# Output copies moved ahead of normalization and decoding in an attention pass, and its small transfers moved from GpSimd's queue to SyncE's

## The chip, the cores and the metric

One core of a Trainium2 chip runs the whole kernel. The metric is device time in microseconds, the median of the runs. TensorE is called PE here, VectorE DVE, ScalarE ACT, GpSimd POOL and SyncE SP, as in the profile.

## The reference

Attention with capped scores over 2 batches, 12 heads, 448 positions and 64 columns a head, and then two feed-forward stages on the 896 by 768 result:

```python
scores = cap * np.tanh(scale * np.matmul(q, k.transpose(0, 1, 3, 2)) / cap)
attn = np.exp(scores - np.max(scores, axis=-1, keepdims=True))
attn = attn / (np.sum(attn, axis=-1, keepdims=True) + 1e-09)
x = heads_side_by_side(np.matmul(attn, v))        # 896 x 768
h = x @ w_in                                      # 768 -> 2048
x = (h * (1.0 / (1.0 + np.exp(-1.702 * h)))) @ w_out
xn = x / np.sqrt(np.mean(x * x, axis=-1, keepdims=True) + 1e-06) * rms_g
g = xn @ w_gate                                   # 768 -> 1536
return (g * (1.0 / (1.0 + np.exp(-g))) * (xn @ w_val)) @ w_out2
```

## The kernel before

The order of the instructions on every engine is the order of the program text, so each engine works through its own list, and one instruction that waits holds up all that stand behind it on that engine.

**Attention.** Two heads make a pair; there are 12 pairs (`NPR`), and the loop over `p` runs 13 times (passes 0 to 12). Pass `p` holds work of several pairs. On PE, in this order: the last 64 rows of the scores of pair p (`scores_last`, L305), the transposes of q and k of pair p+1 (`turn`, L263), most of the product of weights and values of pair p-1 (`pv_main`, L332), the third block of scores of pair p and the first of pair p+1 (`scores`, L295), the end of the product of pair p-1 (`pv_last`, L342), and the second block of scores of pair p+1. ACT takes tanh and exp of each block (`exps`, L317 and L318; `tt` are the large blocks, `tl` the last one). PSUM banks rotate: the tiles `v` of `scores_last` and of the two heads of `pv_main` share two banks, three tiles to a pass. So `scores_last` of a pass waits for the output copy of head 0 of the pass before (`z`, L350, on DVE), and the second head of `pv_main` waits until ACT has taken the tanh of `tl` out of the bank that `scores_last` of the same pass filled.

**Normalization.** The values carry a column of ones, so each output `z` holds the sums of its softmax. `sums` spreads those sums over partitions into `rs` by a DMA; `recips` inverts them on DVE (L364) and, for pairs 0 to 8, writes them to DRAM (`recs`, L367); `spread` reads them back to all partitions of a tile `r` (L382), 224 KB written from 3.5 KB. These three transfers are on POOL's queue for pairs 0 to 8. For pairs 9 to 11 the spreading is a product with `blk` on PE (L386). `normal` (L393, L399, L405) multiplies and splits the result in a high and a low part on DVE. In pass p it is the turn of `recips` and `spread` of pair p-3 and, right behind them, of `normal` of pair p-4, ahead of the output copies of pair p-1 on DVE's list. The spreadings of pairs 9 and 10 share one PSUM tile (`spare`).

**Decoding.** Weights of the feed-forward stages come as raw words (`raw`), and each unit of six blocks is decoded by `square`, `sign`, `mask` on ACT, `mid`, `top`, `low` on DVE, `high_part` on ACT (L158) and `low_part` on DVE (L163). Operations of units 0 to 3 are spread over passes 3 to 12 in the order of the list `early`, two in the middle of a pass and one at its end. `low` of a unit also issues the load of the unit three further on, on SP's queue.

**SP's queue** carries the loads of q, k, v and raw weights.

**Feed-forward stages.** They begin with the columns of batch 0 (L558 to L560) right behind the last product of attention, the spreading of pair 10.

Of the kernel before, what the change touches and what calls it, by code (L numbers as in the profile page):

```python
# [9 lines left out]
F32 = mybir.dt.float32  # L10
F32R = mybir.dt.float32r
# [7 lines left out]
def attn_moe_kernel(  # L19
# [14 lines left out]
    nc = tc.nc  # L34
    B, H, S, D = q.shape
# [8 lines left out]
    NPR = B * NP  # L44
# [120 lines left out]
    def run(op, w):  # L165
        if w < len(units) and (op, w) not in done:
            done.add((op, w))
            op(w)
# [8 lines left out]
    def attention():  # L177
        with ExitStack() as actx:
# [89 lines left out]
            def split_kq(p):  # L268
                t, ts = turned.pop(p)
                if p:  # L270
                    x = ap_.tile([128, 2, 2, S], F32R, tag="x", name="x")
                    xs[p] = [[x[:, a, j] for j in range(2)] for a in range(2)]
                    nc.vector.tensor_copy(x[:, 0], t[:, :, 0:S])  # L273
                    nc.vector.tensor_tensor(out=x[:, 1], in0=t[:, :, 0:S], in1=f(x[:, 0]), op=ALU.subtract)
                    for e in range(2):
                        nc.gpsimd.tensor_copy(kbs[p % 2][half[e], :, half[e]], f(x[half[e], :, 0, 384:S]))
                else:
                    xs[p] = [[ap_.tile([128, S], F32R, name=f"x{a}{j}", bufs=1) for j in range(2)] for a in range(2)]
                    for j in (1, 0):
                        nc.scalar.activation(out=xs[p][0][j], in_=ts[j][:, 0:S], func=AF.Copy)  # L280
                    for j in (1, 0):
                        nc.vector.tensor_tensor(out=xs[p][1][j], in0=ts[j][:, 0:S], in1=f(xs[p][0][j]), op=ALU.subtract)
                    for a in range(2):
                        for e in range(2):
                            nc.gpsimd.tensor_copy(kbs[0][half[e], a, half[e]], f(xs[p][a][0][half[e], 384:S]))
# [3 lines left out]
            def scores(p, c):  # L289

                x = xs[p]
                ps = ps_s.tile([128, 2, 512], F32, tag="s", name="s")
                for n, (a, m) in enumerate(TERMS):
                    for e in range(2):
                        nc.tensor.matmul(  # L295
                            out=ps[:, e, 0:S], lhsT=x[a][0][half[e], c * 128:(c + 1) * 128],
                            rhs=x[m][1][half[e]], start=(n == 0), stop=(n == 2),
                        )
                return ps
# [37 lines left out]
            def pv_last(p):  # L337

                g, i = place[p]
                for e in range(2):  # L340
                    w = ves[g % 2][half[e], i, 2 * e:2 * e + 2]
                    nc.tensor.matmul(  # L342
                        out=opened[p, e][:, 0:S], lhsT=w.rearrange("p h d -> p (h d)"), rhs=pt[p, NC][half[e]],
                        start=False, stop=True,
                    )
                for e in range(2):
                    zt[p, e] = zrp.tile([128, S], F32, tag="z", name="z", bufs=7)
                    ps = opened.pop((p, e))
                    if p < NPR - 1:
                        nc.vector.tensor_copy(zt[p, e], ps[:, 0:S])  # L350
                    else:
                        nc.scalar.activation(out=zt[p, e], in_=ps[:, 0:S], func=AF.Copy)

            def sums(p):
                nr[p] = zrp.tile([128, S // 64], F32, tag="rs", name="rs", bufs=3)
                for e in range(2):

                    (nc.gpsimd if p < NPR - 3 else nc.sync).dma_start(
                        out=nr[p][half[e]], in_=zt[p, e][64 - 64 * e:65 - 64 * e, :].rearrange("o (a n) -> o a n", a=64)
                    )  # L360

            def recips(p):
                rs = nr[p]
                nc.vector.reciprocal(out=rs, in_=rs)  # L364
                if p < NPR - 3:
                    d = dram.tile([2, S], F32, tag="recs", name="recs")
                    nc.gpsimd.dma_start(out=d.rearrange("e s -> (e s)").rearrange("(p n) -> p n", p=128), in_=rs)  # L367
                    nr[p] = d
                else:

                    r = zrp.tile([128, S], F32, tag="r", name="r", bufs=3)
                    nc.vector.tensor_tensor(
                        out=r.rearrange("p (a n) -> p a n", n=7), in0=spr.rearrange("p (a n) -> p a n", n=7),
                        in1=rs.unsqueeze(1).to_broadcast([128, 64, 7]), op=ALU.mult,
                    )
                    nr[p] = r

            def spread(p, bank=None):
                d = nr[p]
                if p < NPR - 3:  # L380
                    r = zrp.tile([128, S], F32, tag="r", name="r", bufs=3)
                    nc.gpsimd.dma_start(out=r, in_=d.unsqueeze(1).to_broadcast([2, 64, S]))  # L382
                    nr[p] = (r, r)
                else:
                    o = bank()
                    nc.tensor.matmul(out=o[:, 0:S], lhsT=blk, rhs=d, start=True, stop=True)  # L386
                    nr[p] = (o[:, 0:S], d)
# [40 lines left out]
            def decode(n):  # L428
                for _ in range(min(n, len(early))):
                    run(*early.popleft())  # L430

            def normal(p):
                norm_mul(p)
                norm_hi(p)
                norm_lo(p)

            spare = []

            def bank():
                if not spare:  # L440
                    spare.append(ps_t.tile([128, 2, 512], F32, tag="t", name="t"))
                    return spare[0][:, 0]
                return spare[0][:, 1]

            nc.vector.reciprocal(out=tsc, in_=capt)
            nc.vector.tensor_scalar(out=tsc, in0=tsc, scalar1=1.0 / float(D) ** 0.5, scalar2=None, op0=ALU.mult)
# [3 lines left out]
            for p in range(NPR + 1):  # L450
# [11 lines left out]
                if 3 <= p < NPR:  # L462
                    recips(p - 3)
                    spread(p - 3)
                if p >= 4:
                    normal(p - 4)
                if p >= 1:
                    pv_main(p - 1)
                if p == NPR:
                    spread(p - 3, bank)  # L470
                    recips(p - 2)
                    normal(p - 3)
                if p > 2:
                    decode(2)
                if p < NPR:
                    exps(p, 2, scores(p, 2))
                if p + 1 < NPR:
# [3 lines left out]
                if p >= 1:  # L481
                    pv_last(p - 1)
                    sums(p - 1)
                if p + 1 < NPR:
                    s1 = scores(p + 1, 1)
                if p > 2:
                    decode(1)
                if p == 0:
                    late_constants()

# [5 lines left out]
                if p in (1, 2, 4):  # L496
                    load_to((1, 2, 4).index(p))
            decode(len(early))
            spread(NPR - 2, bank)
            return recips, spread, norm_mul, norm_hi, norm_lo  # L500

    def rest(recips, spread, norm_mul, norm_hi, norm_lo):
# [366 lines left out]
```

## Time and profile before

| | |
|---|---|
| median of 3 runs | 640.97 us (640.3 to 642.27) |
| the profiled execution | 643.85 us, of which the span of the trace is 642.1 us |
| PE busy over the span | 619.8 us (97%) |
| DVE, ACT, POOL busy | 438.5, 400.3 and 81.5 us |
| PE busy from 0 to 160 us | 141.47 us |

The span is the time of one execution on the core; what lies around it (1.75 us) is start and end. A busy share over the whole span hides that attention (to about 142 us) and the feed-forward stages have different limits, so the two are read apart.

### The profile page before, as it was taken

To read this page: it belongs to the slowest core of one execution; us is meant where nothing else is said; L and a number is where in the kernel's file an instruction comes from. 1 tells how busy PE (TensorE), PEld (TensorE's weight loads), DVE (VectorE), ACT (ScalarE), POOL (GpSimd) and SP (SyncE) were. 2 spreads that over 40 slices of the span, in tenths; PEclk is the share of its full clock that TensorE was granted. 3 is DMA by queue.
4 is the path that set the end of the run, shared out by engine and by line. 5 is a ranking of instruction groups with operands and counts; after the bars stand their busy time and mean duration, and the time that the engine had idled before them with its cause. 6 is when DMAs were issued, how large, how long until landed. Compare 5 with 4: busy or idle time off the path is not lost.

```text
span 642.1 us, 8028 instructions
## 1 busy us (share of the span) xinstructions
PE 619.8 (97%) x3076; PEld 527.7 (82%) x3076; DVE 438.5 (68%) x561; ACT 400.3 (62%) x534; POOL 81.5 (13%) x123
## 2 busy tenths in 40 slices
PE   7998889889999999999999999999999999999997
PEld 4565555448888889899898888899998899999997
DVE  2236655777867555366678889999468888588842
ACT  3789588647977545577777656668445676355500
POOL 4313232200000000000002220220013200023100
PEclk9799899899999999999999999999999999999999
DMA  6745423113433432233343323434323334133012
GB/s 140 171 119 143 125 61 96 28 27 105 156 124 99 147 112 90 94 99 100 108 139 98 102 96 98 149 99 147 92 62 127 113 100 147 54 136 106 1 64 109
DMA packets 85925, 67.18 MB, mean 105 GB/s; under 512 B 39924, under 2 KB 83206, under 8 KB 85888
## 3 DMA queue, kind: packets, MB, share of 16 engines
q1 hardware_dynamic: 80720, 64.28, 33.0%
q0 software_dynamic: 4208, 2.16, 1.3%
q8 instruction: 24, 0.39, 0.3%
q10 hardware_dynamic: 960, 0.23, 0.2%
q14 instruction: 13, 0.11, 0.1%
HBM read 63.80 MB, written 2.78 MB: 104 GB/s over the span
## 4 chain that ended last, share of the span: by engine, by line
PE 82%; DMA 8%; DVE 5%; issue 2%; ACT 2%; SPq 1%; POOL 0%; ACTq 0%; DVEq 0%; POOLq 0%
PE b L559 20%; PE b L560 20%; PE b L558 20%; PE b L763 14%; DMA r<-recs 5%; PE v L332 3%; DVE r L393 1%; PE t L263 1%; DMA recs<-rs 1%; PE v L305 1%; PE s L295 1%; DMA q<-in_q 1%; DVE z L350 1%; SPq L234 1%; DVE x L273 1%
## 5 line engine op out<-in xcount | busy, mean ns | idle before, releaser
L558 PE MATMUL b<-x,ring 128*128 128x512 f32 (+1 forms) x480 | 174.5, 364 | 0.1
L559 PE MATMUL b<-x,ring 128*128 128x512 f32 (+1 forms) x480 | 174.1, 363 | 0.2 <-DVE x L405 0.2
L560 PE MATMUL b<-x,ring 128*128 128x512 f32 (+1 forms) x480 | 174.2, 363 | 0.0
L558 PEld LDWEIGHTS b<-x,ring 128*128 128x128 f32 x480 | 90.1, 188 | 10.6 <-ACT x L401 0.5
L559 PEld LDWEIGHTS b<-x,ring 128*128 128x128 f32 x480 | 90.1, 188 | 10.7 <-DVE x L405 0.5
L560 PEld LDWEIGHTS b<-x,ring 128*128 128x128 f32 x480 | 90.1, 188 | 9.4
L137 DVE SCALAR_TENSOR_TENSOR dec<-raw,dec 128x768 uint32<-128x768 uint32 x68 | 69.7, 1025 | 26.7 <-ACT dec L133 26.4
L763 PE MATMUL b<-ring,uA 128*128 128x384 f32 x504 | 87.8, 334 | 0.0
L763 PEld LDWEIGHTS b<-ring,uA 128*128 128x128 f32 x504 | 87.4, 188 | 0.0
L143 DVE SCALAR_TENSOR_TENSOR dec<-raw,dec 128x768 uint32<-128x768 uint32 x68 | 73.2, 1076 | 1.1
L560 PE MATMUL b<-g,ring 128*128 128x384 f32 (+1 forms) x192 | 70.0, 365 | 0.0
L559 PE MATMUL b<-g,ring 128*128 128x384 f32 (+1 forms) x192 | 69.8, 364 | 0.0
L558 PE MATMUL b<-g,ring 128*128 128x384 f32 (+1 forms) x192 | 69.6, 362 | 0.0
L163 DVE TENSOR_TENSOR ring<-dec,ring 128x768 fp32r<-128x768 f32 x68 | 66.7, 982 | 3.6 <-ACT ring L158 3.6
L158 ACT ACTIVATE ring<-dec 128x768 fp32r<-128x768 f32 x68 | 56.7, 834 | 15.2 <-DVE dec L149 7.0
L149 DVE SCALAR_TENSOR_TENSOR dec<-raw,dec 128x768 uint32<-128x768 uint32 x68 | 64.9, 954 | 1.3
L129 ACT ACTIVATE dec<-dec,edge 128x768 f32<-128x768 f32 x68 | 63.4, 932 | 1.0
L125 ACT ACTIVATE dec<-raw 128x768 f32<-128x768 f32 x68 | 60.9, 896 | 0.5 <-DVE ring L163 0.5
L332 PE MATMUL v<-tt,vn 128*128 128x448 f32 x144 | 59.5, 565 | 0.7 <-DVE z L350 0.7
L133 ACT ACTIVATE dec<-dec 128x768 f32<-128x768 f32 x68 | 57.3, 842 | 1.4
L731 POOL TENSOR_TENSOR a<-a,gg 128x512 f32<-128x512 f32 (+1 forms) x18 | 29.6, 1646 | 188.6 <-DVE gg L724 184.2
L332 PEld LDWEIGHTS v<-tt,vn 128*128 128x128 f32 x144 | 28.2, 203 | 25.6 <-issue 21.9
(102 smaller groups left out, 660.9 us busy)
## 6 DMA issues: line engine op xcount, KB each, us to landing
raw<-in_moe_w_out SPq DMA_DIRECT2D x20, 768.0 KB, 4.2
raw<-in_moe_w_in SPq DMA_DIRECT2D x16, 768.0 KB, 4.7
raw<-in_moe_w_gate SPq DMA_DIRECT2D x12, 768.0 KB, 4.2
raw<-in_moe_w_val SPq DMA_DIRECT2D x12, 768.0 KB, 4.2
raw<-in_moe_w_out SPq DMA_DIRECT2D x8, 512.0 KB, 3.7
out<-oacc SPq DMA_DIRECT2D x6, 384.0 KB, 2.3
raw<-in_moe_w_out SPq DMA_DIRECT2D x8, 256.0 KB, 3.3
r<-recs POOLq DMA_DIRECT2D x9, 224.0 KB, 7.8
```

Of the source, the lines that this page charges most:

```text
L125: nc.scalar.activation(out=f(d), in_=f(r[:, :, 1]), func=AF.Square, scale=2.0 ** 15)
L129: nc.scalar.activation(out=f(d), in_=f(d), func=AF.Sign, bias=edge)
L133: nc.scalar.activation(out=f(d), in_=f(d), func=AF.Relu, scale=2.0 - 2.0 ** -23)
L137: nc.vector.scalar_tensor_tensor(out=d, in0=hi, scalar=3, in1=d, op0=ALU.logical_shift_left, op1=ALU.bitwise_and)
L143: nc.vector.scalar_tensor_tensor(out=d, in0=hi, scalar=0xC0000000, in1=d, op0=ALU.bitwise_and, op1=ALU.bitwise_or)
L149: nc.vector.scalar_tensor_tensor(out=d, in0=lo, scalar=29, in1=d, op0=ALU.logical_shift_right, op1=ALU.bitwise_or)
L163: nc.vector.tensor_tensor(out=t[:, 1], in0=f(d), in1=f(t[:, 0]), op=ALU.subtract)
L332: nc.tensor.matmul(out=ps[:, 0:S], lhsT=w.rearrange("p h d -> p (h d)"), rhs=pt[p, c][:, e], start=(c == 0), stop=False,)
L558: nc.tensor.matmul(out=wide(o, b), lhsT=w0, rhs=x0, start=first, stop=False)
L559: nc.tensor.matmul(out=wide(o, b), lhsT=w0, rhs=x1, start=False, stop=False)
L560: nc.tensor.matmul(out=wide(o, b), lhsT=w1, rhs=x0, start=False, stop=last)
L763: nc.tensor.matmul(out=os_[t][n][:, 0:HW], lhsT=uA[xi][:, i, tok], rhs=w[:, wi, n * HW:(n + 1) * HW], start=(i == 0 and xi == 0 and wi == ...
```

## The change

In each pass from 4 to 11, `normal(p-4)` moves from ahead of `pv_main` to behind the output copies of the pass. Of the three decoding operations of a pass, only those of ACT that stand at the head of the list stay in the middle (`decode_act`); the rest follow at the end, behind `normal`. In pass 12 `normal(8)` and `normal(9)` both come ahead of `recips(10)`. The spreading of pair 9 moves into pass 11 and has a PSUM tile of its own, and so has that of pair 10. The transfers `rs`, `recs` and `r` of all pairs go to SP's queue. The tiles of pair 0's split q and k are taken from the ring of `z`, which has 8 buffers in place of 7. Lines behind 354 stand one number lower in the changed kernel (L393 is L392 there), later ones two higher.

```diff
@@ split_kq, pair 0
-                    xs[p] = [[ap_.tile([128, S], F32R, name=f"x{a}{j}", bufs=1) for j in range(2)] for a in range(2)]
+                    xs[p] = [[zrp.tile([128, S], F32R, tag="z", name="z", bufs=8) for j in range(2)] for a in range(2)]
@@ pv_last
-                    zt[p, e] = zrp.tile([128, S], F32, tag="z", name="z", bufs=7)
+                    zt[p, e] = zrp.tile([128, S], F32, tag="z", name="z", bufs=8)
@@ sums, recips, spread
-                    (nc.gpsimd if p < NPR - 3 else nc.sync).dma_start(
+                    nc.sync.dma_start(
...
-                    nc.gpsimd.dma_start(out=d.rearrange("e s -> (e s)").rearrange("(p n) -> p n", p=128), in_=rs)
+                    nc.sync.dma_start(out=d.rearrange("e s -> (e s)").rearrange("(p n) -> p n", p=128), in_=rs)
...
-                    nc.gpsimd.dma_start(out=r, in_=d.unsqueeze(1).to_broadcast([2, 64, S]))
+                    nc.sync.dma_start(out=r, in_=d.unsqueeze(1).to_broadcast([2, 64, S]))
@@ 
+            def decode_act(n):
+
+                done_ = 0
+                while done_ < n and early and (early[0][0] in ACT_OPS or early[0][0] is high_part):
+                    run(*early.popleft())
+                    done_ += 1
+                return done_
...
-            spare = []
-
-            def bank():
-                if not spare:
-                    spare.append(ps_t.tile([128, 2, 512], F32, tag="t", name="t"))
-                    return spare[0][:, 0]
-                return spare[0][:, 1]
@@ the loop over passes
                 if 3 <= p < NPR:
                     recips(p - 3)
                     spread(p - 3)
-                if p >= 4:
+                if p == NPR:
                     normal(p - 4)
+                    normal(p - 3)
+                    recips(p - 2)
                 if p >= 1:
                     pv_main(p - 1)
-                if p == NPR:
-                    spread(p - 3, bank)
-                    recips(p - 2)
-                    normal(p - 3)
                 if p > 2:
-                    decode(2)
+                    n = decode_act(2)
                 if p < NPR:
                     exps(p, 2, scores(p, 2))
...
                 if p >= 1:
                     pv_last(p - 1)
                     sums(p - 1)
+                if p == NPR - 1:
+                    spread(p - 2, lambda: ps_t.tile([128, 2, 512], F32, tag="t", name="t")[:, 0])
                 if p + 1 < NPR:
                     s1 = scores(p + 1, 1)
+
+                if 4 <= p < NPR:
+                    normal(p - 4)
                 if p > 2:
-                    decode(1)
+                    decode(3 - n)
...
-            spread(NPR - 2, bank)
+            spread(NPR - 2, lambda: ps_s.tile([128, 2, 512], F32, tag="s", name="s")[:, 0])
```

On DVE, pass 8 of the kernel before reads as follows, from the split of q and k of pair 9 (`x<-t`) to the output copies (`z<-v`).

```order
L273 CAST x<-t 128x896
L274 TENSOR_TENSOR x<-t,x 128x896
L364 RECIPROCAL rs<-rs 128x7
L393 TENSOR_TENSOR r<-z,r 64x448 x2
L399 CAST x_66<-r 128x448
L405 TENSOR_TENSOR x_67<-r,x_66 128x448
L149 SCALAR_TENSOR_TENSOR dec<-raw,dec 128x768
L350 COPY z<-v 128x448 x2
```

The same pass of the changed kernel, from the same split:

```order
L273 CAST x<-t 128x896
L274 TENSOR_TENSOR x<-t,x 128x896
L363 RECIPROCAL rs<-rs 128x7
L350 COPY z<-v 128x448 x2
L392 TENSOR_TENSOR r<-z,r 64x448 x2
L398 CAST x_66<-r 128x448
L404 TENSOR_TENSOR x_67<-r,x_66 128x448
L149 SCALAR_TENSOR_TENSOR dec<-raw,dec 128x768
```

The copies now stand ahead of `normal` of pair 4 (`r<-z`, the `CAST`, the subtraction), and `low` of unit 1 (L149), on which ACT's next `high_part` depends, now stands behind both.

On DVE, from the output copies of pair 9 (end of pass 10, before) to `normal` of pair 8 (pass 12):

```order
L350 COPY z<-v 128x448 x2
L149 SCALAR_TENSOR_TENSOR dec<-raw,dec 128x768
L364 RECIPROCAL rs<-rs 128x7
L393 TENSOR_TENSOR r<-z,r 64x448 x2
L399 CAST x_66<-r 128x448
L405 TENSOR_TENSOR x_67<-r,x_66 128x448
L364 RECIPROCAL rs<-rs 128x7
L372 TENSOR_TENSOR r<-spr,rs 128x448
L350 COPY z<-v 128x448 x2
L163 TENSOR_TENSOR ring<-dec,ring 128x768
L393 TENSOR_TENSOR r<-z,r 64x448 x2
L399 CAST x_66<-r 128x448
```

In the changed kernel, from the two decoding operations at the end of pass 10 to `normal` of pair 8:

```order
L143 SCALAR_TENSOR_TENSOR dec<-raw,dec 128x768
L149 SCALAR_TENSOR_TENSOR dec<-raw,dec 128x768
L363 RECIPROCAL rs<-rs 128x7 x2
L371 TENSOR_TENSOR r<-spr,rs 128x448
L350 COPY z<-v 128x448 x2
L392 TENSOR_TENSOR r<-z,r 64x448 x2
L398 CAST x_66<-r 128x448
L404 TENSOR_TENSOR x_67<-r,x_66 128x448
L163 TENSOR_TENSOR ring<-dec,ring 128x768
L392 TENSOR_TENSOR r<-z,r 64x448 x2
L398 CAST x_66<-r 128x448
L404 TENSOR_TENSOR x_67<-r,x_66 128x448
```

The reciprocal of pair 8, from which its `recs` and `r` start, stood right behind one decoding operation and the copies of pair 9; now `normal` of pair 6 and two decoding operations stand between those copies and it. Behind these rows `recips` of pair 10 stood ahead of `normal` of pair 9, and now stands behind it.

On SP, the loads that follow the raw weights of pass 5 in the kernel before are those of q and k for pairs 10 and 11, of pass 6:

```order
L113 DMA raw<-in_moe_w_in 128x6x256 x2
L234 DMA k_104<-in_k 128x4x64 x3
L234 DMA k_104<-in_k 64x4x64
L234 DMA q_105<-in_q 128x4x64 x3
L234 DMA q_105<-in_q 64x4x64
L239 DMA vn_106<-in_v 128x4x64 x3
L243 DMA ve_108<-in_v 64x2x64 x2
```

On SP in the changed kernel, from `recs` and `r` of pair 3 (pass 6) to the second load of q; `DMAHW` with a number is one of eight counters that the transfers of this queue use in turn, and a transfer waits until the last one on its counter has landed:

```order
L366 DMA recs<-rs 128x7 [waits DMAHW0_49,DVE_49]
L381 DMA r<-recs 128x1x448 [waits DMAHW1_49,DMAHW0_49]
L357 DMA rs<-z 64x1x7 [waits DMAHW2_49,DVE_49]
L357 DMA rs<-z 64x1x7 [waits DVE_49]
L234 DMA k_104<-in_k 128x4x64 [waits DMAHW4_49,PE_49]
L234 DMA k_104<-in_k 128x4x64 [waits DMAHW5_49,PE_49]
L234 DMA k_104<-in_k 128x4x64 [waits DMAHW6_49,PE_49]
L234 DMA k_104<-in_k 64x4x64 [waits DMAHW7_49,PE_49]
L234 DMA q_105<-in_q 128x4x64 [waits PE_49]
L234 DMA q_105<-in_q 128x4x64 [waits DMAHW1_49,PE_49]
```

The loads now stand behind `r` of pair 3, and the second load of q uses the counter of that `r` (DMAHW1), so it waits until `r` has landed. `recs` and `r` of pair 4 follow eight transfers behind it.

## Rows read from the trace of the kernel before

**Rows 1.** Windows view (start:end, length, busy us of each engine, PEclk), the rest of the kernel.

```profile
160.00:642.00 482.00, 478.31 (x2443) 438.13 (x2441) 351.65 (x428) 288.51 (x403) 41.31 (x28) 1.00 0.33 106
```

**Rows 2.** Timeline of PE, passes 4 to 12 (start us, us, line, operation, [idle <-releaser]).

```profile
49.71 0.84 PE L305 MATMUL v<-x,kb 128*128 128x448 f32 x3 [0.19 <-DVE z L350]
...
71.77 0.96 PE L305 MATMUL v<-x,kb 128*128 128x448 f32 x3 [2.48 <-DVE z L350]
...
82.64 0.84 PE L305 MATMUL v<-x,kb 128*128 128x448 f32 x3 [0.19 <-DVE z L350]
...
94.01 0.84 PE L305 MATMUL v<-x,kb 128*128 128x448 f32 x3 [2.37 <-DVE z L350]
...
95.56 4.67 PE L332 MATMUL v<-tt,vn 128*128 128x448 f32 x12
...
100.17 1.49 PE L295 MATMUL s<-x 64*128 64x448 f32 x12
...
103.21 0.84 PE L305 MATMUL v<-x,kb 128*128 128x448 f32 x3 [0.19 <-DVE z L350]
...
126.18 0.85 PE L305 MATMUL v<-x,kb 128*128 128x448 f32 x3 [0.20 <-DVE z L350]
...
141.81 1.02 PE L386 MATMUL t<-r,blk 128*128 128x448 f32 x2 [1.52 <-DVE r L393]
...
142.32 0.69 PE L558 MATMUL b<-x,ring 128*128 128x384 f32 x1
```

**Rows 3.** Timeline of DVE, passes 7 to 12.

```profile
76.78 1.20 DVE L393 TENSOR_TENSOR r<-z,r 64x448 f32<-64x448 f32 x2
...
78.99 0.95 DVE L137 SCALAR_TENSOR_TENSOR dec<-raw,dec 128x768 uint32<-128x768 uint32 x1
...
84.46 1.09 DVE L273 CAST x<-t 128x896 fp32r<-128x896 f32 x1 [1.44 <-PE t L263]
...
86.59 0.19 DVE L364 RECIPROCAL rs<-rs 128x7 f32<-128x7 f32 x1
...
89.89 1.26 DVE L393 TENSOR_TENSOR r<-z,r 64x448 f32<-64x448 f32 x2 [3.10 <-DMA r<-recs]
...
102.44 1.16 DVE L350 COPY z<-v 128x448 f32<-128x448 f32 x2 [1.09 <-PE v L342]
...
133.13 1.15 DVE L350 COPY z<-v 128x448 f32<-128x448 f32 x2
...
137.46 1.27 DVE L393 TENSOR_TENSOR r<-z,r 64x448 f32<-64x448 f32 x2 [2.31 <-DMA r<-recs]
...
139.97 0.62 DVE L372 TENSOR_TENSOR r<-spr,rs 128x448 f32<-128x448 f32 x1
```

**Rows 4.** The chain that ended last: reciprocals of pair 8 to DRAM and back.

```profile
127.83 0.57 POOL recs L367
...
130.68 6.76 DMA r<-recs
```

**Rows 5.** Tile r: landing times of the nine spreading transfers.

```profile
DMA to landing us min/median/max: 6.8/7.8/9.8
```

**Rows 6.** DMA view: a load of similar size on SP's queue (KB each, us to landing).

```profile
k<-in_k SPq DMA_DIRECT2D x3, 192.0 KB, 2.9
```

**Rows 7.** Timeline of SP's queue: four loads of q.

```profile
8.35 2.38 SPq L234 DMA_DIRECT2D q<-in_q  x4
```

**Rows 8.** Timeline of ACT, end of pass 8 and start of pass 9.

```profile
103.07 0.83 ACT L158 ACTIVATE ring<-dec 128x768 fp32r<-128x768 f32 x1
...
103.81 0.99 ACT L317 ACTIVATE tt<-s,tsc 128x896 f32<-128x896 f32 x1
...
105.78 0.61 ACT L317 ACTIVATE tl<-v,tsc 128x448 f32<-128x448 f32 x1
```

**Rows 9.** Windows of 2 us after two idle times of PE.

```profile
72.00:74.00 2.00, 2.00 (x10) 1.83 (x10) 1.02 (x2) 1.20 (x2) 0.99 (x2) 0.59 0.15 47
...
94.00:96.00 2.00, 1.99 (x13) 1.73 (x14) 1.43 (x3) 1.08 (x2) 1.06 (x2) 1.00 0.16 50
```

## The prediction

> **What bounds the kernel now.** I first read the windows view by stage: from 160 us to the end PE is busy 478.31 of 482 us at full clock [rows 1], so whatever starts the feed-forward stages later or earlier moves the end by as much. The gain or loss lies in attention. There I read PE's timeline by the start T(p) of a pass, which is its L305 row. Undisturbed, a pass takes 103.21 - 94.01 = 9.20 us. The seven passes 4 to 10 take 126.18 - 49.71 = 76.47 us, 12.07 more than 7 x 9.20 [rows 2]. The reader is to see that every second pass begins with an idle time put down to the output copy `z` (2.48 at 71.77, 2.37 at 94.01), and that the usual one is 0.19. DVE's timeline tells why the copy is late: DVE stood idle 3.10 us at 89.89 for the transfer `r`, at `normal`, which stands ahead of the copies on its list [rows 3]. So the copies wait behind a transfer that they don't need. The chain view prices that transfer for pair 8: 2.85 us from the start of `recs` to that of `r`, and 6.76 until `r` lands [rows 4]; over all nine `r` lands after 6.8 to 9.8 us, with 7.8 in the middle [rows 5].
>
> A part of the 12.07 is clock: pass 6, 71.77 to 82.64, takes 10.87 us though only the usual 0.19 stands at its end, 1.67 more than 9.20 [rows 2]. Behind the 2.48 us of idle time the granted clock of a window was 0.59, so its lower level (1.2 GHz) for most of it; behind 2.37 us it stayed 1.00 [rows 9].
>
> **What the change removes.** With the copies ahead of `normal`, a late `r` no longer delays `scores_last`. `normal` of a pair now starts where the copies end: they start at T+8.43 (102.44 - 94.01) and take 1.16, so at T+9.59, or 0.39 into the next pass [rows 2, 3]. Behind it DVE does `normal` (2.21, 76.78 to 78.99), one or two decodings (0.95 each), the split of the next pair (2.13, 84.46 to 86.59) and the reciprocal (0.19) [rows 3]. With two decodings the split ends at 0.39 + 2.21 + 1.90 + 2.13 = 6.63, and the reciprocal at 6.82. PE wants the split for the second half of its L295 row, at T + 6.16 + 0.75 = 6.9 [rows 2]. That work hides the later split, by only 0.3 us. If `r` comes by the time at which `normal` starts, all seven passes take 9.20: **-12.07 us**.
>
> The deadline of `r`: the reciprocal of pair q in pass q+3 ends at T+6.8 at the latest, and `normal` starts one pass later, at 9.20 + 9.59 = T+18.8. The transfers need 2.85 + 6.76 = 9.6. That holds with 2 us to spare, if SP is free.
>
> **Where SP is not free: pass 7.** What SP's queue costs no row shows for `r`. The bounds are 2.9 us, for a load of 192 KB on that very queue [rows 6], and 9.8, the longest of the nine [rows 5]. I take 6.76, since it is the same transfer, and the same for `recs` (2.85). The order on SP shows that between `r` of pair 3 and `recs` of pair 4 stand two sums, eight loads of q and k and five of v, and that the second load of q waits until `r` of pair 3 has landed. That `r` lands at T(6) + 6.8 + 2.85 + 6.76 = 16.4, which is T(7)+7.2. Eight issues at 0.6 (2.38 for four [rows 7]) follow, so `recs` of pair 4 starts at T(7)+12.0 and its `r` lands at 12.0 + 9.6 = 21.6, **2.8 us late**. In pass 5, two sums, eight loads and one of raw weights stand ahead of `recs` of pair 2 (0.4 + 11 x 0.6 = 7.0, and 7.0 + 9.6 = 16.6): in time. In passes 1 and 2 the loads of raw units 0 and 1 stand behind sums; I take nothing, and 2.9 as their bound.
>
> **A new wait on ACT: pass 9.** `low` of unit 1 now stands behind `normal` of pair 4, and ACT's list has `high_part` of that unit ahead of all exps of pair 9. `normal` starts at T(9) + 0.39 + 2.8 = 3.2; with 2.21 and 0.95 `low` ends at 6.35; `high_part` takes 0.83, the tanh and exp of a block 1.97 (103.81 to 105.78) and the tanh of `tl` 0.61 [rows 8], together T(9)+9.76. PE's second head of `pv_main` needs that tanh; it would start at 1.55 + 4.61/2 = 3.85 [rows 2]. PE waits 9.76 - 3.85 = **5.9 us** (3.1 were `r` in time), and I add 1.67 for the clock, since the wait is longer than 2.48. Queued behind are all of PE's pass and so everything else.
>
> **The end of attention.** The reciprocal of pair 8 now ends at T(11) + 0.39 + 2.21 + 1.90 + 0.19 = 4.7. Its `r` lands at 4.7 + 9.6 = 14.3, where before DVE could go on at 137.46 - 126.18 = 11.28 [rows 2, 3]. Then come `normal` of pairs 8 and 9 (4.42), the reciprocal and L372 of pair 10 (0.81), and L558 follows 0.51 behind the spreading (141.81 to 142.32): T(11)+20.0 against 16.14 before. **+3.9 us.** The tiles of their own do take away the reason of the 1.52 us wait at 141.81 (`normal` of pair 9 reading the other half of the tile), but `normal` of pair 9 now stands ahead of the same spreading on DVE's list, so nothing comes back. Before, PE had worked until 141.81 - 1.52, T+14.1; with one spreading moved out it stops near 13.6 and idles some 6 us: 1.67 more for the clock. What follows on DVE moves by less than PE, so the wait for pair 11 doesn't grow.
>
> At nothing stand the buffers (pair 0's tiles are read last in pass 0 and the ring comes round in pass 3) and POOL's relief (it keeps only small casts; they have until the next pass).
>
> **Sum** against the profiled execution: -12.07 + 5.9 + 1.67 + 3.9 + 1.67 = +1.1, 643.85 to 644.9 us. The median was 640.97, so the same ratio gives 642.0.
>
> **Rule against row, for `r`.** The Trainium skill ("DMA: Bandwidth & Descriptors", section "Why a DMA increments its semaphore by 16 and not by 1") says that a transfer runs on as many engines, at most 16, as divide the outermost dimension of both sides, on the software and the hardware path alike; `r` is read as [2, 64, 448], so on two. At that page's 27 GiB/s an engine and 2 us fixed, an estimate is 6.0 us on SP, and the sum would be -1.2; by the load of 192 KB [rows 6] it would be -4.7. The trace agrees so far as 224 KB took 6.76 with little else to move.
>
> **The rivals.**
> *`r` is fast on SP* (2.9): pair 3's lands at T(7)+3.4, so no load waits; fifteen issues put `recs` of pair 4 at T(7)+9.4, and its `r` comes at 15.2, in time. PE waits 3.1 in pass 9. In pass 12 DVE itself gets to `normal` of pair 8 at 6.95 + 1.15 + 2.21 + 0.95 = 11.3 (from 133.13 [rows 3]), and L558 starts at 17.0, +0.9. -12.07 + 3.1 + 0.9 + 2 x 1.67 = -4.7: 636.3. For it speaks the load's row, against it every row of `r`.
> *`r` is slow* (7.8, the middle of the nine, with loads in front of it): `r` of pair 4 is 4.9 late, PE waits 8.0, the end costs 4.9: +4.2, or 645.1. At 9.8 it would be +10.2, 651.2. It decides for slower from about 7.0 us on (each us of `r` costs three: two in pass 9, one at the end).
> *The clock doesn't fall* in one or both places, as behind the 2.37 us: down to -2.3, 638.7.
>
> **How the numbers follow.** A measurement here can tell about 0.3% (1.9 us) from no change. I give the forecast 0.42, the slow `r` 0.27, the fast one 0.18, the clock 0.13. Faster: the fast `r` and most of the clock, 0.28. Slower: the slow `r` and the upper part of the forecast, 0.40. Same: 0.32. The range leaves out the last piece of the fast and slow ends: 636 to 649; the forecast's own is 639 to 645.
>
> **What would show it.** Right: passes 4 to 8 of 9.2 us; in pass 9 an idle time of PE of 3 us or more ahead of the second head of `pv_main`, put down to ACT; ACT idle for DVE's L149 just before; a PE idle time of 4 us or more ahead of the spreading of pair 10, and DVE idle there for `r`. Wrong: passes 4 to 8 longer than 9.2, PE waiting for the split or for `z`; or `r` landing in 3 us.

## The result and the profile after

The changed kernel takes 649.38 us (median of 4 runs, 647.41 to 651.08), the kernel before on the same chip 641.38 (4 runs, 640.3 to 642.27). That is 8.0 us more, 1.0125 by these two medians; the recorded ratio is 1.0099, with a 95% interval of 1.007 to 1.0129. (The ratios given with the experiments are the recorded ones too; they differ from the quotient of the two medians by up to 0.003.) Either way it is slower by about 1%, where 642.0 was forecast. The time lies at the top of the range: 0.38 us above its 649, which is less than the runs of one kernel differ.

The profiled execution took 649.74 us with a span of 648.0, so 5.9 us more than that of before, where the sum said +1.1. The trace of before is of an execution that took longer (643.85 us) than the four runs above, though over all runs on record that kernel takes 640.0 to 647.3. So the two traces account for 5.9 of the 8.0 us, and the rest is within the spread of single executions.

The timeline of PE in the changed kernel, the starts of passes 7 to 11 (L305), PE's idle times between them, and the last two spreadings of attention:

```profile
76.23 0.85 PE L305 MATMUL v<-x,kb 128*128 128x448 f32 x3 [0.19 <-DVE z L350]
84.61 0.47 PE L295 MATMUL s<-x 64*128 64x448 f32 x2 [1.34 <-DVE x L273]
85.64 0.67 PE L295 MATMUL s<-x 64*128 64x448 f32 x4 [0.57 <-DVE x L274]
88.16 1.49 PE L305 MATMUL v<-x,kb 128*128 128x448 f32 x3
98.40 0.85 PE L305 MATMUL v<-x,kb 128*128 128x448 f32 x3 [0.19 <-DVE z L350]
...
110.06 4.56 PE L332 MATMUL v<-tt,vn 128*128 128x448 f32 x6 [7.67 <-ACT tl L317]
117.58 0.85 PE L305 MATMUL v<-x,kb 128*128 128x448 f32 x3 [0.19 <-DVE z L350]
126.78 0.85 PE L305 MATMUL v<-x,kb 128*128 128x448 f32 x3 [0.19 <-DVE z L350]
...
146.23 1.83 PE L385 MATMUL s<-r,blk 128*128 128x448 f32 x2 [5.42 <-DVE r L371]
147.18 1.20 PE L560 MATMUL b<-x,ring 128*128 128x384 f32 x1
```

The idle times for `z` of [rows 2] are gone: of passes 4 to 10 all but three take 9.20 us. Pass 7 takes 11.93 (PE waits for the split `x`), pass 8 takes 10.24, pass 9 takes 19.18 (PE waits 7.67 for the tanh of `tl`), and PE stands 5.42 us ahead of the spreading of pair 10. What DVE waited for, in its timeline:

```profile
80.25 1.25 DVE L392 TENSOR_TENSOR r<-z,r 64x448 f32<-64x448 f32 x2 [3.63 <-DMA r<-recs]
...
103.43 1.25 DVE L392 TENSOR_TENSOR r<-z,r 64x448 f32<-64x448 f32 x2 [4.64 <-DMA r<-recs]
...
105.68 0.95 DVE L149 SCALAR_TENSOR_TENSOR dec<-raw,dec 128x768 uint32<-128x768 uint32 x1
...
140.72 1.25 DVE L392 TENSOR_TENSOR r<-z,r 64x448 f32<-64x448 f32 x2 [2.21 <-DMA r<-recs]
```

These are the normals of pairs 2, 4 and 8: a late `r` still stops DVE, in the first two cases for longer than in [rows 3], and the split, the decoding and the product of pair 10 are now what stands behind it. ACT's timeline shows the path in pass 9, from L149 on DVE through `high_part` (L158) to the exps:

```profile
106.67 0.84 ACT L158 ACTIVATE ring<-dec 128x768 fp32r<-128x768 f32 x1 [8.32 <-DVE dec L149]
...
109.39 0.61 ACT L317 ACTIVATE tl<-v,tsc 128x448 f32<-128x448 f32 x1
```

Why `r` is late stands in the timeline of SP's queue (start us, duration of the issue):

```profile
59.83 4.64 SPq L234 DMA_DIRECT2D k<-in_k  x4
64.51 2.45 SPq L234 DMA_DIRECT2D q<-in_q  x4
67.00 0.60 SPq L113 DMA_DIRECT2D raw<-in_moe_w_in  x1
67.70 0.49 SPq L366 DMA_DIRECT2D recs<-rs  x1
72.32 0.55 SPq L381 DMA_DIRECT2D r<-recs  x1
...
74.22 0.53 SPq L113 DMA_DIRECT2D raw<-in_moe_w_in  x1
74.84 0.76 SPq L366 DMA_DIRECT2D recs<-rs  x1
82.47 0.54 SPq L381 DMA_DIRECT2D r<-recs  x1
...
94.69 0.54 SPq L366 DMA_DIRECT2D recs<-rs  x1
96.32 0.54 SPq L381 DMA_DIRECT2D r<-recs  x1
...
98.20 0.54 SPq L366 DMA_DIRECT2D recs<-rs  x1
103.96 0.54 SPq L381 DMA_DIRECT2D r<-recs  x1
```

`recs` of pairs 2 and 3 each follow a load of raw weights (768 KB), and `r` can be issued only 4.62 and 7.63 us later; `recs` of pair 4, with no such load ahead, takes 1.63. In [rows 4] it was 2.85. A load is not the only thing that holds `recs` up: that of pair 5 (98.20) has no load of raw weights near it and still takes 5.76 us, until just after `r` of pair 4 has landed (96.32 + 7.09 = 103.41); and `recs` of pair 3 has `r` of pair 2 (72.32 to 80.25) beside it as well as its load. The `r` itself takes about what it took on POOL's queue, 6.8 to 9.8 us in [rows 5]. The chain view has it for pairs 3 and 4:

```profile
82.47 7.37 DMA r<-recs
...
96.32 7.09 DMA r<-recs
```

The granted clock (the third value from the end) in windows of 2 us behind the three stretches of waiting:

```profile
88.00:90.00 2.00, 2.00 (x8) 1.61 (x7) 0.43 (x2) 0.76 (x2) 0.00 (x0) 0.50 0.52 127
...
110.00:112.00 2.00, 1.94 (x3) 1.12 (x4) 0.00 (x0) 1.94 (x4) 0.00 (x0) 0.50 1.10 344
...
148.00:150.00 2.00, 2.00 (x8) 2.00 (x7) 1.96 (x3) 0.00 (x0) 0.00 (x0) 0.50 0.00 0
```

It stood at its lower level (1.2 GHz) in all three, so the clock was paid three times, not twice. By the end the rest of the kernel is as before: PE is busy 484.49 of the last 488 us.

### The profile page after: what moved, and what is told of

Read it like the earlier page. It is cut to its first block, busy times and chain, and to the rows that moved or that the text cites. A ratio compares the mean times of both kernels' runs of the same rounds, so it can differ in the third digit from the quotient of the medians.

```text
span 648.0 us, 8021 instructions
## 1 busy us (share of the span) xinstructions
PE 621.5 (96%) x3076; PEld 528.3 (82%) x3076; DVE 437.8 (68%) x561; ACT 400.2 (62%) x534; POOL 58.2 (9%) x87
## 4 chain that ended last, share of the span: by engine, by line
PE 86%; DMA 7%; DVE 3%; ACT 1%; SPq 1%; issue 1%
PE b L562 21%; PE b L561 21%; PE b L560 21%; PE b L765 13%; PE v L332 5%; DMA r<-recs 3%; PE s L295 2%; DMA recs<-rs 2%; PE v L305 1%; PE t L263 1%; DVE r L392 1%; PE v L342 1%; DVE z L350 1%; DMA q<-in_q 1%; DMA rs<-z 1%
## 5 line engine op out<-in xcount | busy, mean ns | idle before, releaser
L560 PE MATMUL b<-x,ring 128*128 128x512 f32 (+1 forms) x480 | 175.5, 366 | 0.0
L561 PE MATMUL b<-x,ring 128*128 128x512 f32 (+1 forms) x480 | 174.8, 364 | 0.0
L560 PEld LDWEIGHTS b<-x,ring 128*128 128x128 f32 x480 | 90.9, 189 | 10.4 <-issue 0.4
L561 PEld LDWEIGHTS b<-x,ring 128*128 128x128 f32 x480 | 90.7, 189 | 10.4 <-issue 0.6
L158 ACT ACTIVATE ring<-dec 128x768 fp32r<-128x768 f32 x68 | 56.7, 833 | 23.5 <-DVE dec L149 15.3
L561 PE MATMUL b<-g,ring 128*128 128x384 f32 (+1 forms) x192 | 69.9, 364 | 0.0
L560 PE MATMUL b<-g,ring 128*128 128x384 f32 (+1 forms) x192 | 69.6, 362 | 0.0
L149 DVE SCALAR_TENSOR_TENSOR dec<-raw,dec 128x768 uint32<-128x768 uint32 x68 | 64.9, 955 | 1.4
```

The costliest lines, as they stand in the source:

```text
L149: nc.vector.scalar_tensor_tensor(out=d, in0=lo, scalar=29, in1=d, op0=ALU.logical_shift_right, op1=ALU.bitwise_or)
L560: nc.tensor.matmul(out=wide(o, b), lhsT=w0, rhs=x0, start=first, stop=False)
L561: nc.tensor.matmul(out=wide(o, b), lhsT=w0, rhs=x1, start=False, stop=False)
```

## The experiments

All ratios are to the kernel before on the same chip. Its median was 642.76 us beside two of the runs (the halves by columns, and the old order with the halves on SP's queue) and 643.01 beside the eight others, which were taken on two chips.

**The two parts apart.** First the new order with the old queue:

```diff
-                    nc.sync.dma_start(
+                    (nc.gpsimd if p < NPR - 3 else nc.sync).dma_start(
...
-                    nc.sync.dma_start(out=d.rearrange("e s -> (e s)").rearrange("(p n) -> p n", p=128), in_=rs)
+                    nc.gpsimd.dma_start(out=d.rearrange("e s -> (e s)").rearrange("(p n) -> p n", p=128), in_=rs)
...
-                    nc.sync.dma_start(out=r, in_=d.unsqueeze(1).to_broadcast([2, 64, S]))
+                    nc.gpsimd.dma_start(out=r, in_=d.unsqueeze(1).to_broadcast([2, 64, S]))
```

> The changed kernel with rs, recs and r of pairs 0 to 8 back on POOL's queue; its order of work stays. Theory A (the gain of the earlier copies is there, and late transfers on SP plus the new order of high_part and of the end give it back): recs of pairs 2 and 4 no longer stand behind loads, so passes 4 to 8 take 9.2 us each, the wait of PE in pass 9 falls from 7.7 to about 3.1 us (low still stands behind normal), the end of attention stays about as long (20 us from T(11) to the first feed-forward product). About 9 us less than the changed kernel: 640.5, within 0.3% of the kernel before. Theory B (the queue makes no difference, the order alone costs): 649, and the 11.9 us pass 7 and the 7.7 us wait stay.

Measured: 643.92 us, ratio 1.0025 (0.9996 to 1.0055), 3.4 us above the 640.5 of theory A and 5.1 below theory B. Then the old order with the new queue, the same three lines of the kernel before changed to `nc.sync`:

> The kernel before with nothing changed but the queue: rs, recs and r of all pairs on SP. Theory A: normal stands where it stood, with about 4 us less until its deadline than in the changed kernel, so the copies wait longer in the passes whose recs stand behind loads (pairs 1, 2, 4, 6), by 3 to 8 us in two or three of them: 646 to 655, slower than before by 1% or more. Theory B (the queue makes no difference): 641.

Measured: 643.72 us, ratio 1.0022 (0.9997 to 1.0047), where I had expected 646 to 655: a miss. Neither part alone costs anything that can be told; together they cost 1%. PE's idle times in these two runs, first with the new order on POOL's queue, with the starts of passes 9 and 10:

```profile
96.40 0.84 PE L305 MATMUL v<-x,kb 128*128 128x448 f32 x3 [0.21 <-DVE z L350]
...
103.42 4.85 PE L332 MATMUL v<-tt,vn 128*128 128x448 f32 x6 [3.05 <-ACT tl L317]
...
111.86 0.84 PE L305 MATMUL v<-x,kb 128*128 128x448 f32 x3 [0.19 <-DVE z L350]
...
141.11 1.83 PE L385 MATMUL s<-r,blk 128*128 128x448 f32 x2 [6.21 <-DVE r L371]
```

and with the old order on SP's queue:

```profile
83.09 1.46 PE L305 MATMUL v<-x,kb 128*128 128x448 f32 x3 [5.20 <-DVE z L350]
```

With the old queue `r` of pair 4 is in time and the wait of pass 9 is 3.05 us, the 3.1 that the prediction gave for that case. Passes 4 to 10 then take 71.68 us, 4.8 less than before, and the end of attention loses it again (T(11)+21.0 against 16.14). In the old order on SP one pass loses 5.20 us and others gain (two of the later idle times for `z` are 1.71 and 0.89 us): passes 4 to 10 take 75.31 us against 76.47.

**Why `r` is slow.** The changed kernel with `r` read by two transfers, of 64 partitions each:

```diff
-                    nc.sync.dma_start(out=r, in_=d.unsqueeze(1).to_broadcast([2, 64, S]))
+                    for e in range(2):
+                        nc.sync.dma_start(out=r[half[e]], in_=d[e:e + 1, :].to_broadcast([64, S]))
```

> The changed kernel with r read in two transfers of 64 partitions each (one for each head), both on SP; the bytes are the same. Theory A with the rule on the number of engines (two for [2, 64, 448], sixteen for 64 rows): r lands in 3 to 4 us in place of 7.1, pairs 2 and 4 are in time, pass 7 takes 9.2, pass 9 waits about 3.1 us, the end of attention is 3 us shorter: 636 to 639, faster than before. Rival (the source, 3.5 KB of DRAM read 64 times, sets the time of r): r still lands after about 7 us, 649.

Measured: 636.83 us, ratio 0.9914 (0.9887 to 0.9942). `r` lands 2.7 to 3.7 us after its issue, passes 4 to 8 take 9.20 us each, pass 9 takes 13.90. With `r` short, `recs` of pairs 3 and 5 are quicker too, from SP's timeline of this run:

```profile
72.19 0.53 SPq L113 DMA_DIRECT2D raw<-in_moe_w_in  x1
74.17 0.34 SPq L366 DMA_DIRECT2D recs<-rs  x1
77.51 1.80 SPq L382 DMA_DIRECT2D r<-recs  x2
...
93.93 0.54 SPq L366 DMA_DIRECT2D recs<-rs  x1
95.56 1.10 SPq L382 DMA_DIRECT2D r<-recs  x2
```

3.34 us in place of 7.63 for pair 3, though the load of raw weights is there as before, and 1.63 in place of 5.76 for pair 5. So the long `r` held up the next `recs`, and a part of what the load seems to cost is `r`'s. (The two old orders on SP's queue, further up and further down, differ in nothing but the halves: 7.39 and 4.64 us for pair 3.) To tell the shape from the mere number of transfers, the same bytes in two transfers cut by columns, which keep the outermost dimension 2:

```diff
-                    nc.sync.dma_start(out=r, in_=d.unsqueeze(1).to_broadcast([2, 64, S]))
+                    for h in range(2):
+                        hs = slice(h * S // 2, (h + 1) * S // 2)
+                        nc.sync.dma_start(out=r[:, hs], in_=d[:, hs].unsqueeze(1).to_broadcast([2, 64, S // 2]))
```

> The changed kernel, with r read by two transfers again, but cut by columns: each fills all 128 partitions with 224 of the 448 columns, so that each still has the outermost dimension 2 on both sides, where the halves by partitions had 64. Bytes and number of transfers are those of the run with halves by partitions. Theory, that the outermost dimension decides how many engines a transfer runs on: two engines for each, so r lands after some 7 us if both take the same two (646 to 651 us), after 4 to 5 if they take different ones (639 to 645), and the DMA share while r runs is 0.12 or 0.25, not 0.6. Rival, that two transfers in flight were the gain: r lands after 2.7 to 3.7 us again and the time is that of the halves by partitions, 635 to 638.

Measured: 653.51 us, ratio 1.0166 (1.0122 to 1.0209); that is 2.5 us above the range of the theory, whose transfer times came true all the same. The chain view gives 7.06 us for `r` of pair 3 and 6.86 for pair 4. So two transfers are no quicker by themselves, and the DMA share below says that they went through no more engines than one whole transfer. The DMA share (the last column but one) of windows in which `r` of pair 4 runs, first the changed kernel:

```profile
100.00:101.00 1.00, 1.00 (x5) 0.54 (x4) 0.00 (x0) 0.00 (x0) 0.00 (x0) 1.00 0.12 45
101.00:102.00 1.00, 1.00 (x4) 0.38 (x2) 0.00 (x0) 0.00 (x0) 0.00 (x0) 1.00 0.13 50
```

then halves by columns:

```profile
103.00:104.00 1.00, 1.00 (x3) 0.19 (x1) 0.00 (x0) 0.00 (x0) 0.00 (x0) 1.00 0.14 48
104.00:105.00 1.00, 0.08 (x1) 0.00 (x0) 0.00 (x0) 0.00 (x0) 0.00 (x0) 1.00 0.13 47
```

and halves by partitions:

```profile
93.00:94.00 1.00, 1.00 (x12) 0.51 (x8) 0.00 (x0) 0.97 (x2) 0.12 (x1) 1.00 0.65 145
```

0.125 is two of the profile's 16 engines, at 45 to 50 GB/s; with 64 in the outermost dimension the share is 0.65 and the rate three times as high.

**Is the order needed once `r` is quick?** The kernel before with nothing changed but the same two halves, on POOL's queue:

```diff
-                    nc.gpsimd.dma_start(out=r, in_=d.unsqueeze(1).to_broadcast([2, 64, S]))
+                    for e in range(2):
+                        nc.gpsimd.dma_start(out=r[half[e]], in_=d[e:e + 1, :].to_broadcast([64, S]))
```

> The kernel before (profiled 642.1 us span), with r read from recs by two transfers of 64 partitions each in place of one of 2 x 64, still on POOL's queue; nothing else of the change. Theory that the long r was all that the order of DVE's list had to be protected from: r lands in 3 to 4 us after the start of its transfer instead of 6.8 to 9.8, DVE no longer waits 3.1 us at normal, the copies z come on time in the old order too, passes 4 to 10 come down from 76.5 to 65 to 68 us, and the end of attention, which waited for r of pair 8, comes some 3 us earlier: 628 to 632 us. Rival, that on POOL's queue a transfer is limited by what POOL spends on making it: two transfers take as long as one, 641 to 644. Rival, that the old order loses time by itself: r is quick, but z still holds PE by 1 us or more every second pass: 635 to 638.

Measured: 630.61 us, ratio 0.9798 (0.9757 to 0.9838). In the old order `normal` now waits at most 0.39 us, the copies are in time, and passes 4 to 10 take 64.41 us, which is 7 x 9.20. The longest wait of DVE for `r`, and the starts of two passes that began 2.4 us late before [rows 2]:

```profile
81.38 1.27 DVE L394 TENSOR_TENSOR r<-z,r 64x448 f32<-64x448 f32 x2 [0.39 <-DMA r<-recs]
```

```profile
67.65 0.84 PE L305 MATMUL v<-x,kb 128*128 128x448 f32 x3 [0.19 <-DVE z L350]
...
86.05 0.85 PE L305 MATMUL v<-x,kb 128*128 128x448 f32 x3 [0.18 <-DVE z L350]
```

The same with all three transfers on SP's queue (the edits of the second run and the halves):

> The kernel before in its old order, with r in halves and all three transfers on SP's queue: against the changed kernel with halves (636.8 us) it differs by the order and the PSUM tiles alone, against the kernel before with halves (630.6 us) by the queue alone. Theory, that the 6.2 us between these two are the moved decodings (pass 9, 4.7 us) and the longer list of DVE at the end: passes 4 to 10 take 64.4 to 66 us and the time is 630 to 633. Rival, that they come from the loads in front of recs on SP's queue: some passes of 5 to 8 are longer than 9.2 for z again, and the time is 635 to 638.

Measured: 634.64 us, ratio 0.988 (0.9845 to 0.9916), between the two theories. By the medians, which come from different chips, the queue costs 4.0 us (634.64 - 630.61) and the new order 2.2 (636.83 - 634.64); for the second the intervals of the two ratios overlap, so there only the traces speak, one execution of each. The queue's part is all at `normal` of pair 4, whose `recs` stands behind fifteen other issues (two sums, eight loads of q and k, five of v), as the prediction had it for pass 7. DVE waits there, and PE at the start of the next pass:

```profile
94.51 1.27 DVE L394 TENSOR_TENSOR r<-z,r 64x448 f32<-64x448 f32 x2 [4.12 <-DMA r<-recs]
```

```profile
98.42 0.85 PE L305 MATMUL v<-x,kb 128*128 128x448 f32 x3 [3.16 <-DVE z L350]
```

Passes 4 to 10 take 69.12 us here and 69.11 in the new order with the same halves: there the late copies are gone, and the wait for `tl` in pass 9 costs as much. The new order then loses at the end, T(11)+17.74 against 15.01: the first product of the feed-forward stages starts there at 135.85 us (L561 of that kernel) and here at 133.53 (L559).

**What keeps `recs` waiting.** Loads of raw weights of units 2 to 5 on POOL's queue, `recs` and `r` on SP's:

```diff
-                nc.sync.dma_start(out=t[:, b0:b0 + n].rearrange("p k f t -> p k (f t)"), in_=s)
+                (nc.gpsimd if 2 <= w <= 5 else nc.sync).dma_start(out=t[:, b0:b0 + n].rearrange("p k f t -> p k (f t)"), in_=s)
```

> The changed kernel, with the loads of raw weights of units 2 to 5 (768 KB each) issued on POOL's queue instead of SP's; recs and r stay on SP. Theory that recs of pairs 2 and 3 was late because it stood behind a load of raw weights on SP's queue: recs of pair 2 now takes 1.6 to 2.9 us to the start of r instead of 4.6, that of pair 3 the same instead of 7.6, passes 4 to 8 are 9.2 us each, and the wait of pass 9 falls from 7.7 to about 5: 642 to 645 us. Rival, that the load keeps the 16 engines themselves busy whatever queue it is on: recs still takes 4 us or more and passes 7 and 8 stay at 11.9 and 10.2: 648 to 651.

Measured: 649.76 us, ratio 1.0099 (1.0072 to 1.0126), the changed kernel's own. The time is the rival's, so my theory of the queue falls. SP's timeline of this run (a load of raw weights was issued on POOL at 72.17):

```profile
69.11 0.55 SPq L366 DMA_DIRECT2D recs<-rs  x1
71.62 0.55 SPq L381 DMA_DIRECT2D r<-recs  x1
...
73.88 0.34 SPq L366 DMA_DIRECT2D recs<-rs  x1
81.94 0.54 SPq L381 DMA_DIRECT2D r<-recs  x1
```

`recs` of pair 2, with the load no longer in front, takes 2.51 us in place of 4.62; but its `r` now runs beside that load, and DVE waits 4.80 us for it in place of 3.63. `recs` of pair 3 takes 8.06, though no load is ahead of it on its queue; `r` of pair 2 is, which DVE waited for until 81.40, so this number is not the load's alone. What the run shows is that the load costs as much from the other queue as from the same.

**The moved decodings and the end.** The changed kernel with `high_part` of unit 1 behind `mid` of unit 2:

```diff
-                + [(high_part, 1), (mid, 2), (square, 3), (low_part, 1), (top, 2), (sign, 3), (low, 2)]
+                + [(mid, 2), (high_part, 1), (square, 3), (low_part, 1), (top, 2), (sign, 3), (low, 2)]
```

> The changed kernel with two entries of the list early exchanged: high_part of unit 1 comes after mid of unit 2, so it falls into the middle of pass 9 and no longer ahead of the exps of pair 9. Theory A: ACT no longer waits for low there, but normal of pair 4 is still 4.6 us late, and the split of pair 10 stands behind it on DVE, so PE waits some 4 us for the split in place of 7.7 for ACT: 645 to 646. Rival (the order of high_part is the whole of pass 9's loss): the wait goes to zero, about 639 to 640. Rival (it only shows a wait that DVE causes anyway): no change, 649.

Measured: 645.89 us, ratio 1.006 (1.0034 to 1.0085). The wait for `tl` is gone and pass 9 takes 15.02 us in place of 19.18; what is left is the late `r`, which now reaches PE by way of the split:

```profile
106.44 0.72 PE L295 MATMUL s<-x 64*128 64x448 f32 x2 [3.30 <-DVE x L273]
```

The decodings back in the middle of the pass, as before:

```diff
-                    n = decode_act(2)
+                    decode(2)
...
-                    decode(3 - n)
+                    decode(1)
```

> The changed kernel with the decodings where they were before: two in the middle of a pass, one at its end; all else stays changed. Theory that the part of pass 9's wait which isn't r's lateness comes from the moved decodings: behind normal then stands one decoding, not two, so the split ends at T+5.7 in place of T+6.6 and low of unit 1 no longer stands between normal and the exps of pair 9; the wait of pass 9 falls from 7.7 to about 3.5 (the split, behind a late r), but where r is late in pass 7 the two decodings in the middle delay the copies, and z holds PE by 1 to 2 us: 643 to 647 us. Rival: the order of decodings hardly matters, since r's lateness passes to whatever stands behind it: 648 to 651.

Measured: 646.08 us, ratio 1.005 (1.0027 to 1.0073). Pass 9 falls to 13.69 us, and the time lies where I put it, but not for the whole reason: the copies were not delayed in pass 7 (11.04 us, PE waits for `x`), and the end takes 3.6 us longer than in the changed kernel (T(11)+24.0 against 20.40), with PE idle at both late spreadings:

```profile
132.65 1.86 PE L385 MATMUL t<-r,blk 128*128 128x448 f32 x2 [4.79 <-DVE r L371]
...
144.47 0.99 PE L385 MATMUL s<-r,blk 128*128 128x448 f32 x2 [2.28 <-DVE r L371]
```

Last, the changed kernel with `r` in halves, the later `high_part`, and in pass 12 the reciprocal of pair 10 ahead of `normal` of pair 9:

```diff
                     normal(p - 4)
-                    normal(p - 3)
                     recips(p - 2)
+                    normal(p - 3)
```

> The changed kernel with r in halves on SP (636.8 us median when run alone), and two places of the order mended: high_part of unit 1 behind mid of unit 2, so that ACT's exps of pair 9 no longer queue behind low on DVE, and the reciprocal and product of pair 10 ahead of normal of pair 9 in pass 12. Theory: with r in time the later high_part costs nothing, pass 9 falls from 13.9 to 9.2 us (the wait of 2.96 us and the slow clock behind it), and the spreading of pair 10 starts 2.2 us earlier: 629 to 631 us. Rival: the split of the next pair now stands behind two decodings in pass 9 and comes late, as it did in the run with the later high_part alone (3.3 us for x): PE waits 2 to 3 us there and only the end is gained: 633 to 636.

Measured: 631.54 us, ratio 0.9813 (0.9774 to 0.9852), the theory's side, 0.5 us above its range. Passes 4 to 10 take 64.43 us, the first product of the feed-forward stages (L561) follows at T(11)+15.39, and PE's wait ahead of the spreading of pair 10 is 1.06 us. That is as fast as the old order with the halves on POOL's queue (629.71 to 631.74 there, 631.48 to 632.0 here). On SP's queue the old order took 634.64, so there the mended new order is 3.1 us quicker: `normal` of pair 4 stands behind the copies and finds `r` landed, where the old order lost 3.16 us and the clock behind it. On POOL's queue it would have nothing of that kind to win, since the old order's passes take 9.20 us there already; the new order with the halves on POOL's queue was not run. So the halves by themselves reach the best time on record, and with them the whole change needs two mends to come level with it.

## Why the prediction was off

The mechanisms were right: the copies came on time, `r` of pair 4 was late because of what stands ahead of it on SP, the wait passed to `tl` through ACT's list in pass 9, and the end waited for `r` of pair 8. The sizes were not, and one of the prediction's own signs of being wrong appeared: passes 7 and 8 took longer than 9.2 us, in pass 7 with PE waiting for the split. Times of the profiled execution:

| term | forecast | measured |
|---|---|---|
| passes 4 to 8 and 10 at 9.20 us | all | pass 7 +2.73, pass 8 +1.04 |
| pass 9, wait of PE | 5.9 | 7.67 |
| pass 9, clock | 1.67 | 2.31 (19.18 - 9.20 - 7.67) |
| end: L560 after T(11) | 20.0 | 20.40 (147.18 - 126.78) |
| end, clock, up to the last spreading | 1.67 | 2.14 (8.74 against 6.60) |
| start of pass 4 | 0 | -1.08 (48.63 against 49.71) |
| behind the last spreading (L385 at 155.92, L386 at 148.92 before) | 0 | -1.10 (492.08 against 493.18) |

The measured ones add up: -12.07 + 2.73 + 1.04 + 7.67 + 2.31 + 4.26 + 2.14 - 1.08 - 1.10 = +5.9, where 4.26 is 20.40 - 16.14. The last two terms, -2.18 together, were not forecast and are luck as far as the sum goes: pass 4 starts anywhere from 47.78 to 49.71 us in the traces on record, so -1.08 is no effect of the change that they can show. Passes 4 to 10 changed by +1.68 us (78.15 against 76.47) where the forecast had -4.50; that difference of 6.18 is 3.77 in passes 7 and 8 and 2.41 in pass 9.

**The step that failed** is "I take 6.76, since it is the same transfer, and the same for `recs` (2.85)", with "In pass 5 ... in time" as what followed from it. 6.76 for `r` was nearly good: 7.09 for pair 4. The 2.85 was not: beside a load of raw weights it is 4.62 us, and 7.63 beside such a load and the `r` of the pair before (3.34 beside the load with that `r` short). The prediction counted the load as one issue of 0.6 us on the queue, and not as 768 KB on the engines, and it gave `r` no effect on the next `recs` at all. For pair 2 `recs` left at T(5)+9.86 (forecast 7.0: the four loads of k took 4.64 us to issue, not 2.4), took 1.77 longer, and its `r` 1.2 longer: it came at T(5)+22.4 (80.25 - 57.84) against a deadline of 18.8. For pair 3 the same made `r` land at T(6)+22.8 in place of 16.4 and so held back the loads of pass 7 and, through them, pair 4, which was 4.64 late and not 2.8. The rest of pass 9 follows: the 1.8 us by which `r` was later than forecast are the 1.77 by which the wait was longer.

**What held.** The transfer of pair 8: `recs` left at T(11)+4.63 (forecast 4.7), `normal` of pair 8 began at T(11)+13.94 (14.3), with 2.16 us for `recs` in place of 2.85 and 7.15 for `r` in place of 6.76. The deadline, too: with the quick `r`, passes 4 to 8 take 9.20 us. The wait of 3.1 us that pass 9 keeps when `r` is in time was 3.05 and 2.96 in two runs.

**The rule of the Trainium skill** ("DMA: Bandwidth & Descriptors", section "Why a DMA increments its semaphore by 16 and not by 1"), that a transfer runs on the largest number of engines, up to 16, that divides the outermost dimension of both sides, agrees with this case: a share of 0.12 to 0.13 for [2, 64, 448], 7 us for two column halves of the same dimension, and 2.7 to 3.7 for 64 rows. The estimate of 6.0 us from that page's figures, of which the fixed 2 us are given there for GpSimd's queue, was 1.1 short of the 7.09 of pair 4 on SP's. I had used the rule for a price only; read as advice it named the cheaper edit.

**The rivals.** The slow `r` came nearest (+4.2 for 7.8 us), for another reason: not the transfer was slower, but what runs ahead and beside it. The fast `r` on SP did not happen in this shape; with the halves it did. The clock did not stay up.

## What to carry to other kernels

Before you reorder work around a slow transfer, ask why it is slow: its DMA share against its bytes shows on how many engines it runs, and one other shape of it (two transfers of 64 partitions) was worth more here than the whole reordering. A wait that is taken from one consumer goes to the next on the same engine's list, and from there to other engines' lists; follow it until it meets slack. When a small transfer on a deadline moves to a queue with loads, count the loads' bytes as well as their issues, and count what a slow transfer holds up behind it.

## What was not expected of the hardware

A transfer of 3.5 KB (`recs`) took 1.6 to 2.2 us up to the issue of the next in the changed kernel where neither a load of raw weights nor an `r` ran beside it; 5.76 beside a whole `r`, at a DMA share of 0.12 to 0.13, so with most engines free; 3.3 to 5.3 beside a load of 768 KB; and up to 8.1 beside both. That a part of it waits on the two engines of that `r` would explain it, but no view here shows single engines.

Two transfers whose shape gives two engines each took 7.06 us for both, as one whole transfer, at the same share of 0.13.

What the slow clock cost after a wait of PE did not follow the length of the wait. In the changed kernel it was 2.31 us behind 7.67 and 2.14 behind 5.42; before, 1.67 behind 2.48 [rows 2, 9]; but in the new order on POOL's queue 3.21 behind 3.05 (pass 9: 111.86 - 96.40 - 9.20 - 3.05). Nor did the length settle whether the clock fell: in the changed kernel it stood at 0.50 from 88 us on, behind waits of 1.34 and 0.57, and before it stayed at 1.00 behind 2.37 [rows 9].

Which part of the small differences ahead of pass 4 and behind the last spreading (1.1 us each) belongs to the change was not tried, and the ring of 8 buffers and the PSUM tiles of their own were never run without the rest of it.
